# A retention layer with a gated MLP on one core: another hand-written order, and three kinds of copies that may run on GpSimd

## Chip, core and metric

One Trainium2 chip, of which the kernel uses one core. The metric is the device time of one execution in microseconds (us). The kernel before takes 418.49 us (median of three runs, 417.32 to 419.59).

## The reference, cut to what is computed

```python
# retention: batch 4, 8 heads, 768 positions, head size 64
gamma = 1.0 - 2.0 ** (-5.0 - np.arange(H))
for t in range(S):
    state = gamma * state + k[:, :, t] (outer) v[:, :, t]
    y[:, :, t] = D ** -0.5 * q[:, :, t] @ state
x = y laid out as (batch, position, 512)
# gated MLP
h = gelu_tanh(x @ w_in)                  # 512 -> 1024
u, v = h[..., :512], h[..., 512:]
v_n = (v - mean(v)) / sqrt(var(v) + 1e-6) * g_ln
v_s = einsum('ts,bsd->btd', w_sg, v_n) + b_sg[None, :, None]
out = x + (u * v_s) @ w_out
```

`q`, `k`, `v` and the vectors are float32, and three of the weight matrices (`w_in` in two halves, `w_out`) reach the core as 64-bit numbers.

## The kernel before

The work is cut by batch `b` (0 to 3), by half of the sequence `hf` (0 and 1, 384 positions each) and, in the retention, by pair of heads `p` (0 to 3). The retention of one (b, hf, p) goes through six chunks of 64 positions: key times value of each chunk (`D`, a_states), the scan over the chunk states on VectorE (`T`, a_scan, into the tile `sq`), key times query (`S`, a_scores), the mask (`M`, VectorE), the copy of the scanned states beside the queries (`W`, a_beside, two copies of 64 partitions each, into `mw`), the sum of both parts (`O`, a_out), and its scaling into the tile `x` (`X`, a_grow, VectorE). Each result is then split into a high part (`H`, a_hi, a cast) and a low part (`I`, a_lo, a subtraction), so that the MLP can run as three reduced-precision products in place of one. The MLP's steps are `V` and `v` (value half and its gelu), `s`, `N`, `n` (layer norm), `a` and `b` (its high and low parts), `U` and `u` (gate half and its gelu), `G` (the product over positions with `w_sg`), `e`, `m`, `h`, `j` (bias, gate, high and low parts), `Y` (product with `w_out`), `r` and `y` (residual, sum and store).

Weights are prepared on the core: `l` loads a piece, `k`, `b`, `r`, `a` turn a 64-bit piece into float32 (ScalarE, three VectorE instructions, ScalarE, GpSimd), and `h` and `o` split it into a high and a low part. The second letter of such a word names the matrix: `v`, `u` (halves of `w_in`), `o` (`w_out`), `s` (`w_sg`).

No scheduler runs: the list `PROG` is walked word by word, each word issues its step's instructions on their engines, and each engine executes its own in that order. So `X013` is a_grow of batch 0, second half, pair 3, and a last letter D, G or A names VectorE, GpSimd or ScalarE where a step has a choice. `~40` issues 40 matmuls on zeros that keep TensorE busy. All loads and stores are issued by SyncE in the order of `PROG`; the framework gives them eight semaphores in turn, so that each waits for the transfer eight places ahead of it.

Buffers matter in what follows. The PSUM tiles of `D`, `S` and `O` share four buffers; those of the MLP share four others. The tiles `x` and `sq` have one buffer each, so that the next `X` waits for the `I` of the one before, and the next `T` for the `W` of the one before. The key tile of all but the first four pairs has two buffers, so that its load waits for the `D` and `S` of two pairs earlier.

In the kernel before, `P` (scaling of the keys, L242), `W` (L143 by way of L288), `H` (L322) and the high parts of weights (L214) always run on ScalarE.

Of the kernel before, what the change touches and what calls it, by code (L numbers as in the profile page):

```python
# [43 lines left out]
av2 hv0 T000 rv1 W000 lu0 ov0D S001 ls0 bv1 L002 hv2 O000 P001 M001 K000 ov2G C010 D001 L003 ku2 X000 ru2 ~1  # L44
T001 av1 H000 S010 P010 W001 D010 bu2 ~2 L012 kv3 M010 K001 O001 I000G C011 hv1 ~2 T010 lo0 rv3 au2 V0010 lu1
ru3 X001 V0000 H001 bv3 W010 V0020 S011 I001D P011 ov1D O010 ku0 M011 av3 D011 hu2 X010 V0001 ru0 L013 ou2G
T011 H010 V0011 P002 V0021 Q W011 bu0 lo1 D002 I010G S002 hv3 T002 O011 P003 au0 M002 W002 S003 D003 X011 K002
M003 hu0 S012 H011 ou0G O002 T003 ro0 C012 P012 M012 I011G U0000 W003 ov3D D012 X002 K003 ru1 O003 T012 L100
H002 S013 ku1 I002D C013 W012 bu1 V0002 V0012 X003 au1 P013 V0022 M013 H003 D013 ku3 I003D O012 hu1 bu3 L101
ko1 U0001 ro1 X012 au3 ls5 P100 V0013 T013 ls1 H012 V0003 u000 ls6 ou1D v001 V0023 ls10 bo1 W013 lo2 U0010 ls7  # L50
s001 I012G U0020 lo3 v000 v002 ao1 s000 U0011 hs6 s002 hu3 U0021 os6G P101 N00 u001 ou3G ro2 O013 u002 D100
X013 ro3 D101 n000 H013 n001 S100 a000 T100 I013G a001 S101 L102 ko3 M100 b000G U0030 ko0 M101 ko2 ls2 K100
V0120 W100 b001D ls4 U0031 ls3 n002 bo0 L103 a002 V0121 u003 V0100 P102 b002D ls11 V0122 bo2 ls8 V0110 hs3 hs0
V0123 os3D hs2 bo3 V0111 hs9 v012 V0101 hs5 s012 os0G V0112 P103 T101 hs11 V0102 os9G hs1 V0113 hs8 os1D hs7
V0103 os8D v011 U0100 os2D hs4 v010 s011 os11G U0110 hs10 s010 W101 os5G U0120 N01 ao2 U0101 n011 U0121 n012
u010 n010 U0111 os10D a010 os4D u012 b010G U0130 u011 O100 os7G D102 ao0 X100 O101 H100 D103 I100D a011 S102
ao3 X101 ho0 H101 S103 M102 L110 b011G a012 V1020 ho3 M103 U0131 L111 ho1 b012G C110 ho2 V1000 u013 I101D
G0000 oo1D oo3D V1001 P110 oo0G V1021 G0010 K101 oo2G T103 C111 G0001 P111 W103 G0011 K103 G0002 T102 G0012
W102 K102 e000 m000G G0020 e001 m001G h000 G0120 j000G h001 G0021 j001D G0121 r000G G0022 r001G G0122 e002
m002G G0030 r002D h002 O102 j002G D110 X102 O103 H102 T110 D111 I102D S110 W110 X103 S111 M110 L112 H103 V1022  # L60
T111 C113 I103G C112 V1002 L113 M111 W111 G0031 V1023 V1003 v102 G0032 P112 s102 v100 G0100 s100 e003 P113
Y0000 m003G G0110 r003D h003 G0101 j003D Y0001 G0111 y000 G0102 G0112 e010 m010G Y0010 e011 m011G U1000 r010D
# [25 lines left out]
Y2021 M310 W311 V3003 y202 V3011 v300 Y2000 P312 s300 Y2030 P313 Y2001 Y2031 y200 V3012 y203 G2120 V3013 U3000
v301 s301 G2100 G2121 G2101 U3001 G2122 u300 V3020 G2102 V3021 e210 e211 O310 m210D D312 m211D O311 X310 T312
D313 H310 S312 I310D W312 r210D S313 X311 r211G M312 V3022 H311 Y2010 I311D T313 V3023 h210 M313 h211 Y2011  # L90
v302 j211G W313 G2130 s302 j210D U3010 N30 G2131 e212 U3011 n302 n300 G2132 n301 a300 m212D a301 y201 b300G
U3020 a302 e213 u301 Y2130 h212 b301D r212D V3100 b302G V3120 V3101 m213G V3121 j212G h213 U3021 j213D O312
u302 r213G O313 X312 H312 V3110 I312D Y2131 X313 H313 V3102 y213 V3111 I313D V3103 V3112 v310 V3122 s310 V3113
V3123 v311 U3100 s311 v312 s312 Y2120 N31 U3101 Y2121 u310 n312 n310 Y2110 n311 a310 y212 a311 b310G U3030
a312 Y2111 b311D b312G Y2100 y211 U3110 G3010 U3111 G3011 u311 G3030 G3012 G3031 Y2101 G3032 y210 G3000 U3031
G3001 u303 U3120 G3002 U3121 e300 e301 U3130 u312 m300D m301G h300 G3020 r300D h301 U3131 r301D j301D G3021
j300G u313 G3100 G3022 G3101 e302 e303 Y3020 m302D m303G h302 Y3030 r302D h303 G3102 j302G G3120 r303G e310
G3110 m310G G3121 j303G G3111 r310D Y3021 G3122 y302 Y3031 G3112 y303 Y3000 e311 m311D G3130 r311G Y3001 G3131
y300 Y3010 G3132 h310 h311 j310D Y3011 j311D e312 Y3100 e313 m312G y301 Y3120 m313D h312 r312G h313 Y3110
j313D Y3130 j312D r313G Y3121 Y3111 y312 Y3131 y311 Y3101 y313 y310  # L100
# [472 lines left out]
```

## Time and profile before

| | |
|---|---|
| median of three runs | 418.49 us |
| lowest and highest | 417.32 and 419.59 us |
| the profiled execution's own time | 419.46 us |
| span of its profile | 417.7 us |
| busy: TensorE, VectorE, ScalarE, GpSimd | 402.6, 234.4, 173.7, 149.9 us |
| mean granted TensorE clock | 0.988 |
| bytes moved | 41.38 MB |

The span is the time from the first to the last instruction; the 1.8 us between it and the execution's own time lie around it. "Busy" of TensorE counts matmuls from start to a modelled end, so that a busy TensorE need not run at its full rate. In the views, PE is TensorE's matmuls, PEld its weight loads, DVE VectorE, ACT ScalarE, POOL GpSimd, SP SyncE.

### The profile page before, as it was taken

How to read it: one execution, taken by the hardware profiler on the slowest of the kernel's cores; microseconds unless marked ns; L12 is line 12 of the kernel's file. 1: busy time of each engine (PE TensorE's matmuls, PEld its weight loads, DVE VectorE, ACT ScalarE, POOL GpSimd, SP SyncE). 2: the span in 40 equal slices, each digit the busy share in tenths (PEclk: the TensorE clock that was granted, in tenths of full speed). 3: DMA queues.
4: the chain of work that ended last, by engine and by line, in shares of the span. 5: the costliest groups of instructions: out<-in, count | busy, mean ns of one | idle time of the engine just before them, and what ended most of it. 6: DMA issues, size and time to landing. Idle time of an engine off the chain costs nothing.

```text
span 417.7 us, 9358 instructions
## 1 busy us (share of the span) xinstructions
PE 402.6 (96%) x3924; PEld 368.3 (88%) x3924; DVE 234.4 (56%) x461; ACT 173.7 (42%) x306; POOL 149.9 (36%) x148
## 2 busy tenths in 40 slices
PE   8987989969999999999999999999999999999996
PEld 3666878959999999899998999899999998999995
DVE  3897799973453473673454226464272694704453
ACT  4787878454350153544152324355161342201010
POOL 4553244384511513130670471214550042202521
PEclk9999999969999999999999999999999999999999
DMA  8999578040051161415060006225042000100012
GB/s 247 345 288 287 175 250 214 2 134 19 4 151 39 38 176 54 121 32 152 2 184 25 20 0 209 89 83 155 0 126 85 2 19 20 38 20 2 8 58 88
DMA packets 18122, 41.38 MB, mean 99 GB/s; under 512 B 2464, under 2 KB 8096, under 8 KB 18080
## 3 DMA queue, kind: packets, MB, share of 16 engines
q1 hardware_dynamic: 17936, 40.51, 32.4%
q8 instruction: 31, 0.51, 0.6%
q10 hardware_dynamic: 144, 0.27, 0.2%
q14 instruction: 11, 0.09, 0.1%
HBM read 34.48 MB, written 6.29 MB: 98 GB/s over the span
## 4 chain that ended last, share of the span: by engine, by line
PE 79%; DMA 8%; DVE 7%; issue 3%; POOL 1%; SPq 1%; ACT 0%; DVEq 0%; POOLq 0%
PE ps L412 24%; PE py L450 16%; PE pu L395 13%; PE pv L339 13%; PE po L306 5%; PE sc L263 4%; PE ds L255 4%; DMA kt<-in_kk_dram 3%; DMA raw<-in_w_v_dram 2%; DMA raw<-in_w_sg_dram 2%; DMA mw<-in_qv_dram 2%; POOL ws L218 1%; DVE mw L281 1%; DVE wx L179 1%; DVE wx L178 1%
## 5 line engine op out<-in xcount | busy, mean ns | idle before, releaser
L412 PE MATMUL ps<-ws,vh 128*128 128x384 f32 x576 | 106.9, 335 | 0.0
L412 PEld LDWEIGHTS ps<-ws,vh 128*128 128x128 f32 x576 | 100.8, 188 | 1.2
L339 PE MATMUL pv<-wv,xh 128*128 128x512 f32 x288 | 76.1, 402 | 0.0
L395 PE MATMUL pu<-xh,wu 128*128 128x384 f32 x384 | 75.5, 345 | 0.0
L450 PE MATMUL py<-gh,wo 128*128 128x384 f32 x384 | 73.5, 337 | 0.0
L395 PEld LDWEIGHTS pu<-xh,wu 128*128 128x128 f32 x384 | 69.5, 192 | 1.9 <-ACT v L349 0.4
L450 PEld LDWEIGHTS py<-gh,wo 128*128 128x128 f32 x384 | 67.1, 188 | 1.6 <-DVE o L465 0.2
L339 PEld LDWEIGHTS pv<-wv,xh 128*128 128x128 f32 x288 | 53.4, 190 | 10.5 <-ACT v L349 0.5
L143 ACT COPY mw<-sq 64x320 f32<-64x320 f32 (+1 forms) x64 | 52.6, 821 | 20.8 <-DVE sq L268 20.2
L422 DVE SCALAR_TENSOR_TENSOR gt<-ps,gb 128x384 f32<-128x384 f32 x32 | 19.1, 613 | 52.1 <-PE ps L412 49.9
L385 POOL TENSOR_TENSOR vh<-v,vh 128x512 fp32r<-128x512 f32 x19 | 25.0, 1341 | 57.1 <-ACT vh L381 57.1
L433 POOL TENSOR_TENSOR gt<-gt,u 128x384 f32<-128x384 f32 x23 | 24.6, 1073 | 54.6 <-DVE gt L422 54.5
L437 ACT CAST gh<-gt 128x384 fp32r<-128x384 f32 x32 | 16.4, 513 | 63.5 <-POOL gt L433 32.8
L281 DVE TENSOR_TENSOR mw<-sc,tab 64x384 f32<-64x384 f32 x64 | 35.5, 555 | 8.2 <-PE sc L263 5.1
L465 DVE TENSOR_TENSOR o<-py,o 128x384 f32<-128x384 f32 x32 | 17.3, 551 | 33.9 <-PE py L450 28.6
L263 PE MATMUL sc<-mw,kt 64*64 64x64 f32 x768 | 28.0, 222 | 7.3 <-DVE x L313 5.6
L405 ACT ACTIVATE u<-pu 128x384 f32<-128x384 f32 x32 | 15.3, 487 | 44.9 <-PE pu L395 44.6
L263 PEld LDWEIGHTS sc<-mw,kt 64*64 64x64 f32 x768 | 25.3, 137 | 9.8 <-DVE x L313 6.0
L268 DVE TENSOR_TENSOR_SCAN sq<-step,ds 128x384 f32<-128x384 f32 x32 | 30.2, 943 | 6.0 <-PE ds L255 4.1
L306 PEld LDWEIGHTS po<-mw 128*64 128x64 f32 (+1 forms) x768 | 27.0, 139 | 7.1 <-issue 4.7
L306 PE MATMUL po<-mw 128*64 128x64 f32 (+1 forms) x768 | 32.2, 229 | 0.9 <-issue 0.8
L313 DVE TENSOR_TENSOR x<-po,tab 128x384 f32<-128x384 f32 x32 | 17.6, 551 | 27.3 <-PE po L306 24.4
(56 smaller groups left out, 393.2 us busy)
## 6 DMA issues: line engine op xcount, KB each, us to landing
kt<-in_kk_dram SPq DMA_DIRECT2D x32, 384.0 KB, 5.0
mw<-in_qv_dram SPq DMA_DIRECT2D x64, 192.0 KB, 5.4
out_dram<-o SPq DMA_DIRECT2D x32, 192.0 KB, 1.8
raw<-in_w_sg_dram SPq DMA_DIRECT2D x12, 192.0 KB, 4.7
raw<-in_w_v_dram SPq DMA_DIRECT2D x4, 512.0 KB, 7.0
...
```

Of the source, the lines that this page charges most:

```text
L143: nc.scalar.copy(out=out, in_=in_)
L263: mm(out=scs[u][o, c], lhsT=kt[i, c], rhs=mv[j][i, c], start=True, stop=True)
L268: nc.vector.tensor_tensor_scan(out=sqs[u].rearrange("p e c -> p (e c)"), data0=step_t[:, p].rearrange("p e c -> p (e c)"), data1=dss.pop(u ...
L281: nc.vector.tensor_tensor(out=mv[j][h], in0=sc[h], in1=mask_t[h, p : p + 1, :].to_broadcast([64, NCH, C]), op=ALU.mult,)
L306: mm(out=pos[u][o, c], lhsT=w[j][i, c], rhs=mv[j][i, c], start=True, stop=True)
L339: mm(out=pv[b, hf, k], lhsT=x[:, p, a, k * 128 : (k + 1) * 128], rhs=wv_t[:, w, p], start=(p == 0 and n == 0), stop=(p == NP - 1 and n == 2),)
L385: engines[e].tensor_tensor(out=h[:, 1], in0=vt.pop((b, hf, k)), in1=h[:, 0].bitcast(F32), op=ALU.subtract)
L395: mm(out=pu[b, hf, f], lhsT=wu_t[:, w, f, p * 128 : (p + 1) * 128], rhs=x[:, p, a], start=(n == 0), stop=(n == 11),)
L412: mm(out=ps[b, hf, d], lhsT=vh[b, t][:, v, d * 128 : (d + 1) * 128], rhs=ws_t[hf * NT + t][:, w], start=(n == 0), stop=(n == 3 * NT - 1),)
L422: nc.vector.scalar_tensor_tensor(out=t, in0=ps.pop((b, hf, d)), scalar=g_t[:, d : d + 1], in1=b_t[:, hf * HT : (hf + 1) * HT], op0=ALU.mul ...
L433: engines[e].tensor_tensor(out=t, in0=t, in1=ut.pop((b, hf, d)), op=ALU.mult)
L450: mm(out=py[b, hf, c], lhsT=wo_t[c][:, w, d * 128 : (d + 1) * 128], rhs=gh[b, hf, d][:, a], start=(d == 0 and n == 0), stop=(d == 3 and n ...
```

## The change

`PROG` is a new list with the same steps and the same tile sizes: each matmul, load and vector operation of before is in it once. Five places of matmuls on zeros hold 40, 9, 8, 1 and 10 in place of 40, 7, 1, 2 and 2. `P`, `W`, `H` and the weights' `h` now carry an engine. Of 32 key scalings 6 go to GpSimd, of 64 half copies `W` (now one word for each half) 20, of 32 `H` 10, of the weights' 24 high parts 4. Steps that had a choice before are dealt out anew: on VectorE now stand 14 `I` (13 before), 12 `b` (5), 14 `m` (9), 19 `j` (11), 16 `r` (14), 9 low parts of `w_sg` (6), 3 of the gate half (1) and 2 of the value half (3), with the rest of each on GpSimd. A step `Z`, which would issue half a load from ScalarE's queue, is written but stands nowhere in the list.

```diff
-~40 lv0 R lv2 L000 lv1 L001 rv0 kv0 rv2 bv0 lu2 kv2 L010 bv2 ls9 P000 S000 av0 lv3 D000 lu3 M000 kv1 ~7 L011
+~40 lv0 R lv2 L000 lv3 L001 rv0 kv2 rv2 bv2 L010 kv0 bv0 P000A lu2 S000 av2 D000 M000 kv3 ~9 av0 rv3 T000 L011
...
+ON_ACT = {tuple(int(c) for c in w[1:]) for w in PROG if w[0] == "Z"}
...
-    def w_hi(m, i):
+    def w_hi(m, i, e):
...
-        nc.scalar.copy(out=w_parts(m, i)[0], in_=wx[m, i])
+        copy(e, w_parts(m, i)[0], wx[m, i])
...
-        for j, m in enumerate((m0, m1)):
-            h = slice(64 * j, 64 * j + 64)
-            nc.sync.dma_start(out=m[h].rearrange("p a c t -> p (a c t)"), in_=qv[b, hf, p, h])
+        ms[u] = m0, m1
+        for j in (0,) if u in ON_ACT else (0, 1):
+            a_load_half(nc.sync, j, *u)
...
-    def a_keys(*u):
-        ks = kts[u][1]
-        nc.scalar.activation(out=ks, in_=ks, func=AF.Copy, scale=vec_t[:, 0, u[2] : u[2] + 1])
+    def a_load_half(queue, j, b, hf, p):
+        h = slice(64 * j, 64 * j + 64)
+        queue.dma_start(out=ms[b, hf, p][j][h].rearrange("p a c t -> p (a c t)"), in_=qv[b, hf, p, h])
+
+    def a_load_rest(*u):
+        a_load_half(nc.scalar, 1, *u)
+
+    def a_keys(b, hf, p, e):
+        ks, by = kts[b, hf, p][1], vec_t[:, 0, p : p + 1]
+        if e == "A":
+            nc.scalar.activation(out=ks, in_=ks, func=AF.Copy, scale=by)
+        else:
+            engines[e].tensor_scalar(out=ks, in0=ks, scalar1=by, scalar2=None, op0=ALU.mult)
...
-    def a_beside(b, hf, p, e="A"):
-        u = b, hf, p
-        for j in range(2):
-            h = slice(64 * j, 64 * j + 64)
-            copy(e, mws[u][1][j][h, 1 - hf :].rearrange("p c e -> p e c"), sqs[u][h, :, : NCH - 1 + hf])
+    def a_beside(b, hf, p, j, e):
+        u, h = (b, hf, p), slice(64 * j, 64 * j + 64)
+        copy(e, mws[u][1][j][h, 1 - hf :].rearrange("p c e -> p e c"), sqs[u][h, :, : NCH - 1 + hf])
...
-    def a_hi(*u):
-        b, hf, p = u
-        nc.scalar.copy(out=xn[b, hf][:, p, 0], in_=xs[u])
+    def a_hi(b, hf, p, e):
+        copy(e, xn[b, hf][:, p, 0], xs[b, hf, p])
```

Three places of the new order matter below.

The first is SyncE's queue, from the load of pair (0, 1, 2) on (`kt` holds keys, `mw` queries and values, `raw` weights, and `gb` the gate's constants). Before:

```order
L233 DMA kt_334<-in_kk_dram 128x768
L236 DMA mw_335<-in_qv_dram 64x768
L236 DMA mw_336<-in_qv_dram 64x768
L164 DMA raw_367<-in_w_out_dram 128x512
L164 DMA raw_375<-in_w_u_dram 128x512
L233 DMA kt_446<-in_kk_dram 128x768
L236 DMA mw_447<-in_qv_dram 64x768
L236 DMA mw_448<-in_qv_dram 64x768
L490 DMA gb_71<-in_gb_dram 128x772
L164 DMA raw_469<-in_w_out_dram 128x512
```

The same place in the changed kernel, where L238 and L247 are the lines of `kt` and `mw`, and L169 that of weights:

```order
L238 DMA kt_414<-in_kk_dram 128x768
L247 DMA mw_415<-in_qv_dram 64x768
L247 DMA mw_416<-in_qv_dram 64x768
L238 DMA kt_441<-in_kk_dram 128x768
L247 DMA mw_442<-in_qv_dram 64x768
L247 DMA mw_443<-in_qv_dram 64x768
L169 DMA raw_495<-in_w_sg_dram 128x384
L169 DMA raw_513<-in_w_out_dram 128x512
L169 DMA raw_534<-in_w_u_dram 128x512
L238 DMA kt_648<-in_kk_dram 128x768
```

The load of the last pair of batch 0 has moved ahead of two 512 KB pieces of weights.

The second place is VectorE around `X013` (its row is `x<-po`), whose reading of PSUM frees the buffer that `S101` on TensorE takes. Before:

```order
L370 SCALAR_TENSOR_TENSOR lny_805<-lnt_806,lny_805 128x3
L313 TENSOR_TENSOR x_851<-po_823,tab_70 128x384
L375 TENSOR_SCALAR v_776<-v_776,mvar_764,lny_805 128x512
L375 TENSOR_SCALAR v_740<-v_740,mvar_764,lny_805 128x512
L268 SCALAR_TENSOR_TENSOR sq_885<-step_75,ds_838 128x384
L281 TENSOR_TENSOR mw_631<-sc_870,tab_70 64x384
```

After (`lny` is the last instruction of the layer norm's 12 small ones, `v` are its `n`, `wx` the conversion of two pieces of `w_out`, `ws` a low part of `w_sg`):

```order
L382 SCALAR_TENSOR_TENSOR lny_820<-lnt_821,lny_820 128x3
L387 TENSOR_SCALAR v_788<-v_788,mvar_775,lny_820 128x512
L387 TENSOR_SCALAR v_771<-v_771,mvar_775,lny_820 128x512
L387 TENSOR_SCALAR v_763<-v_763,mvar_775,lny_820 128x512
L183 TENSOR_SCALAR wx_852<-wx_852 128x512
L184 TENSOR_SCALAR wx_852<-wx_852 128x512
L187 SCALAR_TENSOR_TENSOR wx_852<-raw_737,wx_852 128x512
L183 TENSOR_SCALAR wx_869<-wx_869 128x512
L184 TENSOR_SCALAR wx_869<-wx_869 128x512
L187 SCALAR_TENSOR_TENSOR wx_869<-raw_731,wx_869 128x512
L223 TENSOR_TENSOR ws_877<-raw_495,ws_877 128x384
L326 TENSOR_TENSOR x_917<-po_884,tab_70 128x384
```

Three `n`, six conversions and one low part of `w_sg` now stand between the small ones and `X013`, where before nothing did.

The third place is VectorE at `X100` and `X101`, the first and second pair of batch 1. Before:

```order
L313 TENSOR_TENSOR x_1162<-po_1133,tab_70 128x384
L326 TENSOR_TENSOR xh_1161<-x_1162,xh_1161 128x384
L313 TENSOR_TENSOR x_1208<-po_1164,tab_70 128x384
L281 TENSOR_TENSOR mw_904<-sc_1194,tab_70 64x384
L281 TENSOR_TENSOR mw_905<-sc_1194,tab_70 64x384
L281 TENSOR_TENSOR mw_950<-sc_1213,tab_70 64x384
L281 TENSOR_TENSOR mw_951<-sc_1213,tab_70 64x384
L326 TENSOR_TENSOR xh_1161<-x_1208,xh_1161 128x384
```

After (L326 is now the line of `X`, L283 that of the scan `T`, here `T102`, L397 the norm's low parts `b`, L338 `I100`, L296 the masks):

```order
L326 TENSOR_TENSOR x_1193<-po_1160,tab_70 128x384
L283 SCALAR_TENSOR_TENSOR sq_1210<-step_75,ds_1177 128x384
L397 TENSOR_TENSOR vh_1227<-v_1046,vh_1227 128x512
L397 TENSOR_TENSOR vh_1195<-v_1069,vh_1195 128x512
L338 TENSOR_TENSOR xh_1192<-x_1193,xh_1192 128x384
L296 TENSOR_TENSOR mw_997<-sc_1245,tab_70 64x384
L296 TENSOR_TENSOR mw_998<-sc_1245,tab_70 64x384
L326 TENSOR_TENSOR x_1290<-po_1197,tab_70 128x384
```

The scan `T102` has moved up to right behind `X100`, and `S103` on TensorE, which took the PSUM buffer that `X101` frees, now takes the one that `T102` frees.

## Rows read from the trace of the kernel before

**Rows 1.** The page: span and busy time of each engine.

```profile
span 417.7 us, 9358 instructions
PE 402.6 (96%) x3924; PEld 368.3 (88%) x3924; DVE 234.4 (56%) x461; ACT 173.7 (42%) x306; POOL 149.9 (36%) x148
```

**Rows 2.** Busy time by stretch: PE, PEld, DVE, ACT, POOL; clock, DMA share, GB/s.

```profile
0.00:85.27 85.27, 77.03 (x966) 60.69 (x966) 69.85 (x133) 60.11 (x107) 36.77 (x39) 0.98 0.75 221
85.27:94.94 9.67, 6.61 (x61) 5.92 (x62) 6.83 (x10) 5.03 (x12) 9.67 (x9) 0.65 0.57 165
94.94:144.93 49.99, 49.99 (x387) 47.88 (x385) 22.17 (x37) 15.83 (x28) 17.27 (x18) 1.00 0.16 49
144.93:413.98 269.05, 268.94 (x2514) 253.82 (x2513) 134.99 (x283) 92.70 (x161) 86.18 (x85) 1.00 0.23 67
```

**Rows 3.** Timeline of TensorE: start, length, instruction [idle before, what ended it].

```profile
32.17 0.91 PE L255 MATMUL ds<-mw,kt 64*64 64x64 f32 x24 [1.39 <-DMA mw<-in_qv_dram]
...
61.89 0.92 PE L263 MATMUL sc<-mw,kt 64*64 64x64 f32 x24 [1.58 <-DVE x L313]
...
85.32 0.92 PE L263 MATMUL sc<-mw,kt 64*64 64x64 f32 x24 [1.00 <-DVE x L313]
89.24 1.54 PE L263 MATMUL sc<-mw,kt 64*64 64x64 f32 x24 [3.01 <-DVE x L313]
...
94.94 0.34 PE L412 MATMUL ps<-ws,vh 128*128 128x384 f32 x1
```

**Rows 4.** Timelines of VectorE and ScalarE around `X013`, `X100` and `X101`.

```profile
61.28 0.56 DVE L313 TENSOR_TENSOR x<-po,tab 128x384 f32<-128x384 f32 x1
...
84.72 0.55 DVE L313 TENSOR_TENSOR x<-po,tab 128x384 f32<-128x384 f32 x1
...
86.91 0.51 ACT L322 CAST xh<-x 128x384 fp32r<-128x384 f32 x1 [1.57 <-POOL ws L218]
...
87.45 1.07 DVE L326 TENSOR_TENSOR xh<-x,xh 128x384 fp32r<-128x384 f32 x1 [2.19 <-ACT xh L322]
88.63 0.56 DVE L313 TENSOR_TENSOR x<-po,tab 128x384 f32<-128x384 f32 x1
```

**Rows 5.** Groups up to 85.27 us: busy us, mean ns | idle before, what ended it.

```profile
L339 PE MATMUL pv<-wv,xh 128*128 128x512 f32 x72 | 18.1, 400 | 0.0
L281 DVE TENSOR_TENSOR mw<-sc,tab 64x384 f32<-64x384 f32 x20 | 11.1, 555 | 3.0 <-DMA mw<-in_qv_dram 1.6 <-PE sc L263 0.9
L268 DVE TENSOR_TENSOR_SCAN sq<-step,ds 128x384 f32<-128x384 f32 x10 | 9.4, 942 | 2.8 <-PE ds L255 2.6
L178 DVE TENSOR_SCALAR wx<-wx 128x512 f32<-128x512 f32 x12 | 6.6, 553 | 6.0 <-ACT wx L170 6.0
L313 DVE TENSOR_TENSOR x<-po,tab 128x384 f32<-128x384 f32 x9 | 4.9, 544 | 0.9 <-PE po L306 0.9
L218 DVE TENSOR_TENSOR ws<-raw,ws 128x384 fp32r<-128x384 f32 x6 | 3.5, 620 | 0.0
L326 DVE TENSOR_TENSOR xh<-x,xh 128x384 fp32r<-128x384 f32 x3 | 1.6, 541 | 0.0
```

**Rows 6.** Groups over the whole span: copies, and the matmuls of `G`.

```profile
L412 PE MATMUL ps<-ws,vh 128*128 128x384 f32 x576 | 106.9, 335 | 0.0
...
L143 ACT COPY mw<-sq 64x384 f32<-64x384 f32 x32 | 28.2, 880 | 7.9 <-DVE sq L268 7.5
...
L145 POOL COPY cy<-sq 128x64 f32<-128x64 f32 x16 | 6.3, 393 | 17.1 <-DVE sq L268 17.0
...
L484 POOL COPY step<-tab 128x1280 f32<-128x1280 f32 x1 | 1.3, 1258 | 4.0 <-DMA tab<-in_c_tab_dram 4.0
```

**Rows 7.** Timeline of GpSimd and VectorE, 9 to 11 us, and VectorE 8.

```profile
7.75 0.43 DVE L179 TENSOR_SCALAR wx<-wx 128x512 int32<-128x512 int32 x1
...
9.04 1.41 POOL L197 TENSOR_TENSOR wx<-wx,raw 128x512 int32<-128x512 int32 x1 [1.60 <-DVE wx L182]
...
9.33 1.40 DVE L179 TENSOR_SCALAR wx<-wx 128x512 int32<-128x512 int32 x1
```

More of the change, by code (lines that the diff above doesn't have):

```diff
@@ L42 @@
 PROG = """
-~40 lv0 R lv2 L000 lv1 L001 rv0 kv0 rv2 bv0 lu2 kv2 L010 bv2 ls9 P000 S000 av0 lv3 D000 lu3 M000 kv1 ~7 L011
[L44 to L62, printed above, removed]
@@ L88 @@
[L88 to L97, printed above, removed]
@@ L98 @@
[L98 to L100 removed]
+~40 lv0 R lv2 L000 lv3 L001 rv0 kv2 rv2 bv2 L010 kv0 bv0 P000A lu2 S000 av2 D000 M000 kv3 ~9 av0 rv3 T000 L011
+hv2A W0000A bv3 hv0A lv1 S001 P001A ov0D W0001A D001 ls10 ov2G M001 O000 lu0 av3 X000 P010A lu3 S010 H000A ~8
@@ new lines @@
+K000 hv3A M010 ku2 ov3G T001 ru2 L002 C010 bu2 D010 W0011A ~1 P011A S011 I000D W0010A K001 L003 V0000 au2 M011
+C011 kv1 V0010 rv1 T010 V0020 hu2A bv1 W0100A D011 O001 ku0 ou2D L012 ~10 ru0 bu0 ru3 ku3 X001 av1 W0101A L013
+P002A S002 T011 H001G hv1A D002 M002 W0111A au0 O010 ls0 W0110A I001D hu0A S003 lo3 ov1D P003A O011 X010 ou0G
+lu1 T002 H010A D003 I010G M003 W0020A U0000 W0021A bu3 V0001 P012A V0021 X011 K002 au3 V0011 C012 T003 H011A
+P013A S012 W0030A I011D O002 W0031G M012 hu3A D012 ro3 K003 S013 X002 L100 C013 ou3D H002A O003 ku1 T012 I002G
@@ new lines @@
+D013 ru1 ls9 M013 W0120G W0121A V0012 ls5 ls11 X003 V0002 L101 bu1 H003A V0022 O012 I003D lo2 T013 au1 P100A
+lo0 U0001 hs9A ls4 X012 W0131A hs0G V0023 ls1 ls6 hu1A V0013 os9D v002 V0003 ou1D ls8 v001 s002 os0G U0100
+u000 ls3 v000 s001 hs5G U0010 H012A ls2 s000 P101A W0130A I012D U0020 lo1 N00 os5G ro2 U0030 ro0 ls7 n000
+U0011 ko0 n001 a000 n002 U0031 bo0 a001 ko2 U0021 hs3A bo2 hs11A O013 u003 hs1A os3D D100 hs10A X013 b000G
+u002 D101 H013A T100 S100 hs4A b001G hs2A S101 u001 M100 L102 ko1 K100 V0120 ko3 ao2 M101 V0110 L103 ro1 V0121
@@ new lines @@
+hs8A I013D a002 os1D V0111 Q hs6A os10D V0122 hs7A b002D W1001A U0101 os7D os4D P102A V0123 bo1 u010 V0112
+v012 os8D V0100 W1000A s012 os2G V0113 T101 P103A V0101 ao1 v011 U0110 W1011A s011 K101 ho1A ao0 V0102 W1010A
+U0120 os11D os6D V0103 bo3 U0130 v010 s010 ho0G U0121 N01 U0131 oo1G u012 U0111 u013 n011 n012 O100 u011 n010
+ao3 D102 a010 X100 a011 O101 T102 H100A b010G D103 a012 ho2A S102 b012D S103 b011D L110 I100D G0020 M103 ho3G
+L111 G0000 X101 C110 oo0G M102 C111 G0021 oo3D G0001 H101G G0022 P110A oo2D G0002 I101G V1020 K102 e000 W1021G
@@ new lines @@
+G0010 P111A m000D V1021 W1020G h000 G0011 j000D T103 r000G V1000 G0012 W1031A K103 W1030G V1001 e001 e002 O102
+m001G D110 X102 m002G h001 O103 T110 D111 H102G h002 S110 W1100A j001D S111 W1101G M110 L112 G0030 M111 j002G
+C113 L113 G0110 T111 I102G C112 G0031 W1110A r001D X103 r002G W1111A V1022 V1002 H103G G0032 P112G G0111 e003
+I103D Y0000 m003G P113A V1023 h003 r003G V1003 v102 j003G G0112 s102 v100 s100 Y0001 G0100 y000 G0120 G0101
+G0121 G0102 G0122 e010 e011 U1000 m010D m011D Y0010 r010D r011G U1001 G0130 u100 Y0020 Y0011 Y0021 y001 V1010
@@ L218, in w_lo @@
         engines[e].tensor_tensor(out=lo, in0=wx.pop((m, i)), in1=hi.bitcast(F32), op=ALU.subtract)
-    kts, mws, dss, scs, sqs, pos, carry, xs, xn = {}, {}, {}, {}, {}, {}, {}, {}, {}
+    kts, mws, dss, scs, sqs, pos, carry, xs, xn, ms = ({} for _ in range(10))
     def a_load(*u):
```

66 lines of the change are left out of this document (40 added, 26 removed).

## The prediction

> **What bounds the kernel now.** I read first the page, then the busy time by stretch, then the timelines around TensorE's waits. On the page [rows 1] TensorE is busy for 402.6 of 417.7 us, so at most some 15 us of plain waiting are there to win. The stretches say where [rows 2]: from 94.94 us to 413.98 it is busy for all but 0.1 us, so that whatever ScalarE, VectorE or GpSimd do better there can hardly show. The waiting lies in the first 94.94 us: 8.2 us up to 85.27 (85.27 - 77.03) and 3.1 us in the next 9.67. In these same 9.67 us the mean granted clock is 0.65, which is a mix of the 2.4 and the 1.2 GHz level; TensorE had stood idle for 3 us just before [rows 3].
>
> In that first part VectorE is the engine that others wait for. It is busy for 69.85 of 85.27 us, ScalarE for 60.11, GpSimd for 36.77 [rows 2]. TensorE's scores wait for VectorE's `x` at 61.89, 85.32 and 89.24 [rows 3], that is for `X013`, `X100` and `X101`, which end at 61.84, 85.27 and 89.19 [rows 4] and free PSUM buffers. The third is the dearest: `X101` could not run until `I100` had left the single `x` buffer, `I100` waited 2.19 us for ScalarE's `H100`, and that stood until a low part of `w_sg` on GpSimd had freed the tile it writes [rows 4]. Once, at 32.17, TensorE waits for a load [rows 3].
>
> A point at which both orders can be compared is the start of the first `G`. Before, it is at 94.94. The changed order has by then done the same matmuls, but for `V1020` and `V1000` (six of 512 columns, which at 18.1 us for 72 [rows 5] are 1.5 us) and with 16 more on zeros. So the changed kernel gains as much as its first `G` starts before 93.4 us.
>
> **The change, part by part.** *VectorE up to `X100`.* Counted word by word, the new order puts three more `I` (541 ns) and three more low parts of `w_sg` (620 ns) ahead of `X100` [rows 5]; one more low part of a 512-wide weight and one less of the norm's cancel. That is 1.6 + 1.9 = 3.5 us more, 73.4 busy in place of 69.85. Its idle time was 15.4 us: 6.0 before the first conversion, 3.0 before masks, 2.8 before scans, 0.9 before `X` [rows 5], and so 2.7 at the very start and in small pieces. The 6.0, the 2.7 and 1.6 of the masks' (a load) stay: 10.3. The other 5.1 were spent where VectorE had run out of work while the loads of pairs (0,1,2) and (0,1,3) and their copies came in. The new order asks for these before 1 MB of other weights, and puts two conversions, three `n` and two low parts of `w_sg`, which came after `X013`, ahead of it. I let 3.5 of the 5.1 go: 11.9 idle. `X100` then ends at 73.4 + 11.9 = 85.3, where it was. The ends are 83.7 (all 5.1 gone) and 88.8 (15.4 as before).
>
> *From `X100` to the first `G`.* `S102` still takes `X100`'s buffer, but `S103` now takes that of `T102`, which stands right behind `X100`: 942 ns [rows 5]. So `T102` ends at 86.2, `S103` runs for 0.9 us as at 85.32 [rows 3], and `G` starts at 87.1, against 93.4: a gain of 6.3 us, between 7.9 and 2.8 at the two ends. `X101`, `H101` (now GpSimd) and `I101` move behind, beside six parts of `G`. Nothing of the clock is counted beyond this; it comes with the hole.
>
> *Copies off ScalarE.* 20 half copies at 880 ns or less [rows 6], 6 scalings, 10 high parts and 4 of weights leave ScalarE, some 27 us. By themselves I cost them at nothing: ScalarE is busy for 60 of 85 us and far less later [rows 2], and no wait of TensorE in rows 3 is for it. What hides them is VectorE's longer queue. Were ScalarE's copies in the way after all, a pair of halves split over two engines would take one copy's time in place of two, 0.9 us less; up to `X100` that is `W003` and `W012`, 1.8 us.
>
> *Copies on GpSimd.* No row shows a half copy there. 1280 elements took 1258 ns in line, 64 strided ones out of the same `sq` 393 ns [rows 6]. For 384 elements that is 0.38 us at one end and 2.36 at the other; I take 1.0, in the middle by ratio, since a half copy reads in line and writes with a stride. The tightest early place is `O103`: GpSimd has `H101`, `I101`, `W1021`, `W1020`, then, as `sq` has one buffer, `T103` on VectorE, and `W1030`. With `X101` at about 89.8 (`T102`, two norm parts, `I100`, one mask pair and itself) and 1.0 to 1.1 each, `W1030` ends at about 97; TensorE comes to `O103` after nine parts of `G` (six matmuls at 106.9/576 us [rows 6], 1.1 each), 12 matmuls of `V` at 0.25 and two small steps, at 101 to 102. At 2.36 a copy this slack of four us is just used up. In the last batch `D313` and `O313` have come within 6 us of each other, with two GpSimd copies, a high and a low part between. For these and other places I take 1.5 us of loss after the first `G`, within -1 (the busy rows hide small waits, so a little could be won) and 4.
>
> *The zeros.* 16 more matmuls at about 0.25 us, as for the 512 columns of `V` [rows 5], are 4 us, ahead of `S001`, `D010` and `S002`, where TensorE waits for copies or for the load that it waits for at 32.17 [rows 3]. Up to `S102` TensorE has 8.2 us to spare [rows 2]; these 4 and one part of `U` that came later before (1.2) leave 3. I cost them at nothing; if that cover goes they cost up to 4.
>
> *Loads.* SyncE already waits for the transfer eight places ahead, in both orders, so no more are open; `Z` is not in the list. What is moved is worth what stands under VectorE's idle time. Behind the load of (1,0,0), which waits for `D012`, now stand three `w_sg` pieces, and behind (1,0,1), which waits for `D013`, two `w_out` pieces whose conversion stands ahead of `X013`.
>
> Sum: -6.3 + 1.5 = -4.8 us. The profiled execution took 419.46 us (span 417.7, 1.8 around it) and would take 414.7; it is 1.0 above the median of 418.49, so the median comes to **413.7 us**.
>
> **The rivals.** *A, larger gain.* VectorE's idle time falls to 10.3 and it is held up less by GpSimd, which has some three two-input operations less ahead of `X100`; one such cost it 0.97 us (1.40 against 0.43 [rows 7]). `X100` then ends at 83.7 - 2.2 = 81.5, which is as early as TensorE can follow, `G` starts at 83.3 and 10 us are won: 408.5. For it: the copies of a pair now run on two engines. Against it: 3 us more on the engine that bounds.
>
> *B, given back.* The work put ahead of `X013` only makes `S101` wait longer, VectorE idles as before, `X100` ends at 88.8, 2.8 us are won and 2 lost in the later places: 417.7. For it: VectorE does not get shorter work, and `w_out` now lies behind `D013`.
>
> *C, slower: GpSimd's copies hold VectorE.* While GpSimd added, a VectorE instruction of 0.43 us took 1.40 [rows 7]. If each moved copy does this too, the six ahead of `X100` (`H001`, `W0031`, `W0120`, `hs0`, `hs5`, `ho0`) cost 5.8 us: `X100` at 91.1, `G` at 92.9, 0.5 won; with half copies near 2.36 us, `O103` and the last batch lose 3.5. That is 421.5. It decides from about 1 us of hold for each copy and 2 us for the copy itself. Against it: the one copy in line [rows 6] is fast. The Trainium skill (GPSIMD Engine Reference, Key points) says that GpSimd shares its SBUF interfaces with VectorE and contends with VectorE instructions that use both ports or have two SBUF inputs; by that rule C's hold is real, the sum would be 421.5, and the pair in rows 7 agrees with it for a GpSimd addition, while no run here shows it for a copy.
>
> **How the numbers follow.** Forecast 0.45 (411 to 416.4 of its own), A 0.15, B 0.25, C 0.15. The range has to take in most of B, A at its edge and the nearer part of C: 408.5 to 420. Over 0.5% (2.1 us, about what a measurement of this kernel can tell from no change) means under 416.4 or over 420.6. Faster: nearly all of the forecast, A and a little of B, 0.61; same: most of B and the edge of C, 0.24; slower 0.15.
>
> **What would show it.** In the changed profile `X013` should end later than 61.84 and `S101` wait for it longer than 1.58 us, `X100` end near 85, `S103` no longer wait for `X101`, `G` start near 87 without a stretch at clock 0.65 before it, and TensorE be busy throughout from there. A half copy on GpSimd near 1.0 us confirms that price; above 2, or VectorE's sum up to `X100` above 76 us, speaks for C. The forecast is wrong if `X100` ends after 89, or if over 3 us are lost after the first `G`.

## The result and the profile after

The changed kernel takes **414.71 us** (median of four runs, 414.46 to 414.90) against 418.85 us for the kernel before on the same chip (417.32 to 419.59, four runs). The ratio is 0.9905, with a 95% interval from 0.9876 to 0.9935: faster by 0.95%, where 413.7 us was forecast. The profiled execution took 414.86 us, its span is 413.1 us. When the changed kernel ran again beside later experiments, one of its seven executions took 436.19 us at a mean granted clock of 0.852; the row "changed, again" below leaves it out, and its trace serves only to show how far two traces of one kernel differ (its `X100` ends at 85.13).

The page of the changed kernel, beside [rows 1]: VectorE's busy time has grown by 12.7 us, ScalarE's has shrunk by 27.1.

```profile
span 413.1 us, 9386 instructions
PE 400.7 (97%) x3937; PEld 366.1 (89%) x3940; DVE 247.1 (60%) x488; ACT 146.6 (35%) x266; POOL 155.2 (38%) x161
```

Busy time by stretch, columns as in [rows 2]. The cuts are the end of `X100` (87.30), the first `G` (89.05) and the start of `O110` (140.54):

```profile
0.00:87.30 87.30, 79.54 (x985) 61.54 (x988) 72.39 (x140) 57.92 (x104) 39.46 (x43) 1.00 0.73 217
87.30:89.05 1.75, 1.70 (x48) 1.56 (x48) 0.94 (x2) 1.75 (x5) 1.49 (x2) 1.00 0.00 0
89.05:140.54 51.49, 51.49 (x395) 49.18 (x391) 27.87 (x46) 12.28 (x23) 27.14 (x28) 1.00 0.26 78
140.54:413.00 272.46, 267.98 (x2514) 253.86 (x2513) 145.87 (x303) 74.62 (x136) 87.16 (x89) 1.00 0.22 68
```

The stretch from `X100` to the first `G`, 9.67 us at a granted clock of 0.65 before [rows 2], is now 1.75 us at 1.00. The stretch ahead of it is longer in this trace: `X100` ends at 87.30 in place of 85.27. That difference is no larger than the one between two traces of the changed kernel (87.30 and 85.13).

TensorE's timeline at `S100` and `S101`, and at `S102`, `S103` and the first `G` (columns as in [rows 3]):

```profile
62.45 0.87 PE L278 MATMUL sc<-mw,kt 64*64 64x64 f32 x24
66.23 0.91 PE L278 MATMUL sc<-mw,kt 64*64 64x64 f32 x24 [2.91 <-DVE x L326]
...
87.35 1.77 PE L278 MATMUL sc<-mw,kt 64*64 64x64 f32 x48 [0.70 <-DVE x L326]
89.05 3.21 PE L424 MATMUL ps<-ws,vh 128*128 128x384 f32 x17
```

VectorE's timeline at `X013`, and at `X100`, `T102` and what follows:

```profile
65.62 0.55 DVE L326 TENSOR_TENSOR x<-po,tab 128x384 f32<-128x384 f32 x1
...
86.75 0.55 DVE L326 TENSOR_TENSOR x<-po,tab 128x384 f32<-128x384 f32 x1
87.21 0.94 DVE L283 TENSOR_TENSOR_SCAN sq<-step,ds 128x384 f32<-128x384 f32 x1
88.97 2.66 DVE L397 TENSOR_TENSOR vh<-v,vh 128x512 fp32r<-128x512 f32 x2 [0.81 <-ACT vh L393]
```

`S102` and `S103` are one row of 48 matmuls now. `S103` follows `T102` and no longer `X101`. `S101` waits longer than in [rows 3], 2.91 us in place of 1.58, for the later `X013`.

VectorE's waits up to the end of `X100`, longest sums first, in the kernel before and then in the changed one (instruction, what it waited for: us in total, times, longest):

```profile
DVE wx L178 <- ACT wx L170: 6.0, 1, 6.0
DVE sq L268 <- PE ds L255: 2.6, 2, 2.4
DVE mw L281 <- DMA mw<-in_qv_dram: 1.6, 1, 1.6
DVE mw L281 <- PE sc L263: 0.9, 1, 0.9
```

```profile
DVE wx L183 <- ACT wx L175: 6.8, 1, 6.8
DVE mw L296 <- PE sc L278: 3.5, 5, 1.6
...
DVE ws L223 <- ACT ws L148: 0.7, 1, 0.7
DVE wu L223 <- ACT wu L148: 0.5, 1, 0.5
```

The waits of the scans and of the load are gone. The wait for TensorE's scores has grown from 0.9 to 3.5 us, and waits of 1.2 us for high parts made by ScalarE have come up. Idle time is 15.4 us before (85.27 - 69.85) and 14.9 after (87.30 - 72.39).

### The profile page after: what moved, and what is told of

The parts are those of the page before. It is cut to its first block, busy times and chain, and to the rows that moved or that the text cites. A ratio compares the mean times of both kernels' runs of the same rounds, so it can differ in the third digit from the quotient of the medians.

```text
span 413.1 us, 9386 instructions
## 1 busy us (share of the span) xinstructions
PE 400.7 (97%) x3937; PEld 366.1 (89%) x3940; DVE 247.1 (60%) x488; ACT 146.6 (35%) x266; POOL 155.2 (38%) x161
## 4 chain that ended last, share of the span: by engine, by line
PE 78%; DVE 9%; DMA 9%; issue 1%; ACT 1%; SPq 0%; ACTq 0%
PE ps L424 24%; PE py L462 16%; PE pv L351 13%; PE pu L407 13%; PE po L319 5%; DMA mw<-in_qv_dram 5%; PE sc L278 4%; PE ds L270 4%; DMA raw<-in_w_v_dram 2%; DMA tab<-in_c_tab_dram 1%; DMA raw<-in_w_sg_dram 1%; DVE ws L223 1%; DVE st L365 1%; DVE wx L187 1%; DVE mw L296 1%
## 5 line engine op out<-in xcount | busy, mean ns | idle before, releaser
L424 PE MATMUL ps<-ws,vh 128*128 128x384 f32 x576 | 105.7, 336 | 0.0
L407 PE MATMUL pu<-xh,wu 128*128 128x384 f32 x384 | 73.0, 339 | 1.6 <-DVE gt L434 1.1
L351 PE MATMUL pv<-wv,xh 128*128 128x512 f32 x288 | 74.1, 396 | 0.0
L462 PE MATMUL py<-gh,wo 128*128 128x384 f32 x384 | 72.1, 336 | 0.0
L407 PEld LDWEIGHTS pu<-xh,wu 128*128 128x128 f32 x384 | 67.5, 188 | 3.8 <-DVE gt L434 1.4
L148 ACT COPY mw<-sq 64x320 f32<-64x320 f32 (+1 forms) x44 | 36.2, 822 | 29.9 <-DVE sq L283 29.6
L296 DVE TENSOR_TENSOR mw<-sc,tab 64x384 f32<-64x384 f32 x64 | 35.5, 555 | 9.4 <-PE sc L278 7.9
L365 DVE BATCH_NORM_STATS2 st<-v 128x6 f32<-128x512 f32 x24 | 16.4, 683 | 31.4 <-ACT v L361 31.4
L473 POOL TENSOR_TENSOR o<-xh 128x384 f32<-128x384 f32 x16 | 18.0, 1125 | 40.6 <-DVE gt L445 40.3
L326 DVE TENSOR_TENSOR x<-po,tab 128x384 f32<-128x384 f32 x32 | 17.6, 549 | 25.0 <-PE po L319 20.4
L283 DVE TENSOR_TENSOR_SCAN sq<-step,ds 128x384 f32<-128x384 f32 x32 | 30.1, 941 | 2.3 <-PE ds L270 1.6
L445 POOL TENSOR_TENSOR gt<-gt,u 128x384 f32<-128x384 f32 x18 | 19.2, 1071 | 31.7 <-DVE gt L434 31.7
L319 PE MATMUL po<-mw 128*64 128x64 f32 (+1 forms) x768 | 31.0, 226 | 0.0
```

Of the source, the lines that this page charges most:

```text
L148: nc.scalar.copy(out=out, in_=in_)
L283: nc.vector.tensor_tensor_scan(out=sqs[u].rearrange("p e c -> p (e c)"), data0=step_t[:, p].rearrange("p e c -> p (e c)"), data1=dss.pop(u ...
L296: nc.vector.tensor_tensor(out=mv[j][h], in0=sc[h], in1=mask_t[h, p : p + 1, :].to_broadcast([64, NCH, C]), op=ALU.mult,)
L319: mm(out=pos[u][o, c], lhsT=w[j][i, c], rhs=mv[j][i, c], start=True, stop=True)
L351: mm(out=pv[b, hf, k], lhsT=x[:, p, a, k * 128 : (k + 1) * 128], rhs=wv_t[:, w, p], start=(p == 0 and n == 0), stop=(p == NP - 1 and n == 2),)
L365: nc.vector.bn_stats(out=st, in_=vt[b, hf, k])
```

## The experiments

The ratio is against runs of the kernel before on the same chip; e1 to e4 shared one chip, e5 to e8 another, and e9 to e11 a third, on which the changed kernel ran again. "Stretch" is worked out from the trace: for each form of VectorE instruction I took the duration that only a tenth of its instructions undercut, over all these traces, and summed what the instructions up to `X100` took beyond it. A trace is one execution of a kernel whose runs lie up to 5 us apart, so times of `G` and `X100` tell apart less finely than they look: the two traces of the changed kernel have `X100` 2.2 us apart. The four traces of the new order with `X100` ahead of 86 us (e1, e4, e9, e10) are of the fastest or the second fastest of six executions each, so that an early `X100` need not be the work of the edit.

| run | ratio to before (95%) | median us | first `G` | `X100` ends | VectorE busy up to `X100` | stretch |
|---|---|---|---|---|---|---|
| before | 1 | 418.85 | 94.94 | 85.27 | 69.85 | 9.9 |
| changed | 0.9905 (0.9876-0.9935) | 414.71 | 89.05 | 87.30 | 72.39 | 9.9 |
| changed, again | 0.9901 (0.9866-0.9936) | 414.28 | - | - | - | - |
| e1 copies back | 0.9837 (0.9802-0.9871) | 413.71 | 87.46 | 85.70 | 70.89 | 8.4 |
| e2 scan early | 0.9992 (0.9960-1.0023) | 419.70 | 96.78 | 86.59 | 71.49 | 11.5 |
| e3 scan late | 1.0005 (0.9977-1.0034) | 420.68 | 93.75 | 86.78 | 72.36 | 9.7 |
| e4 weights late | 0.9895 (0.9849-0.9941) | 415.36 | 87.47 | 85.71 | 70.31 | 7.6 |
| e5 more on VectorE | 0.9943 (0.9917-0.9969) | 417.19 | 92.15 | 90.29 | 75.12 | 10.5 |
| e6 more on ScalarE | 0.9903 (0.9875-0.9931) | 415.29 | 89.92 | 88.16 | 72.33 | 9.9 |
| e7 zeros back | 0.9899 (0.9868-0.9931) | 414.80 | 88.78 | 86.91 | 72.89 | 10.3 |
| e8 low parts to GpSimd | 0.9918 (0.9886-0.9949) | 415.52 | 90.03 | 88.27 | 72.78 | 12.0 |
| e9 load late | 0.9908 (0.9872-0.9944) | 415.06 | 87.84 | 85.98 | 71.20 | 8.6 |
| e10 to VectorE | 0.9907 (0.9871-0.9944) | 415.22 | 86.76 | 85.00 | 71.20 | 5.8 |
| e11 together | 0.9881 (0.9848-0.9914) | 413.92 | 88.13 | 86.37 | 69.61 | 5.2 |

> The changed kernel once more, as the row that the other runs of this chip stand beside: 413.9 to 415.5 us, first chunk product within 1 us of 89 us.

### The third place, undone and alone: e3 and e2

```diff
-X100 a011 O101 T102 H100A b010G D103 a012 ho2A S102 b012D S103 b011D L110 I100D G0020 M103 ho3G L111 G0000 X101 C110
+X100 a011 O101 H100A b010G D103 a012 ho2A S102 b012D b011D L110 I100D X101 S103 T102 G0020 M103 ho3G L111 G0000 C110
```

> The changed kernel with the third place undone: T102 stands behind the high and low parts of chunk 100 again, and S103 waits for X101. Theory: S103 starts near 92.8 us in place of 88.2, the first chunk product near 93.6 in place of 89.05, time 4 to 5 us above the changed kernel (about 419 us). Rival (what S103 waits for is hidden by zeros or caught up later): time within 1 us of the changed kernel.

The ratio is 0.010 above the changed kernel's, some 4.2 us, as the theory has it (by the medians, of two chips, it is 6.0 us): with everything else of the change left in, the whole gain is gone. TensorE of e3 and its second stretch, columns as above:

```profile
92.27 1.55 PE L277 MATMUL sc<-mw,kt 64*64 64x64 f32 x24 [4.25 <-DVE x L325]
93.75 4.43 PE L423 MATMUL ps<-ws,vh 128*128 128x384 f32 x16
```

```profile
86.78:93.75 6.97, 2.71 (x69) 2.46 (x63) 4.52 (x6) 2.38 (x6) 4.88 (x5) 0.73 0.37 116
```

`S103` waits 4.25 us for `X101`, and behind that idle time it runs in 1.55 us in place of 0.87 to 0.91: the granted clock of the stretch is 0.73, a mix of the 2.4 and the 1.2 GHz level.

e2 is the counterpart: the order of before with one thing moved.

```diff
-X100 O101 H100 ... K101 oo2G T103 ... G0002 T102 G0012 W102 K102 e000
+X100 K101 T102 O101 H100 ... oo2G W102 K102 T103 ... G0002 G0012 e000
```

> The order of the kernel before, with one thing from the change: the keys of the last scan step and the step itself (T102) stand right behind X100, ahead of X101. Theory (the third place alone brings a part of the gain, since S103 then takes the buffer that T102 leaves and not the one that X101 leaves): S103 2 to 4 us earlier, time 414.5 to 417 us. Rival (the order of these few steps is worth nothing, the earlier X100 or the clock brings all): time within 0.7 us of the kernel before.

The rival's number came, but not for its reason. VectorE of e2 at `X100` and `T102`, then its GpSimd:

```profile
86.04 0.55 DVE L312 TENSOR_TENSOR x<-po,tab 128x384 f32<-128x384 f32 x1
89.70 0.95 DVE L267 TENSOR_TENSOR_SCAN sq<-step,ds 128x384 f32<-128x384 f32 x1 [3.11 <-POOL cy L144]
```

```profile
85.97 1.28 POOL L384 TENSOR_TENSOR vh<-v,vh 128x512 fp32r<-128x512 f32 x1 [9.86 <-ACT vh L380]
87.21 0.99 POOL L217 TENSOR_TENSOR ws<-raw,ws 128x384 fp32r<-128x384 f32 x1
88.16 1.28 POOL L196 TENSOR_TENSOR wx<-wx,raw 128x512 int32<-128x512 int32 x1
89.38 0.29 POOL L144 COPY cy<-sq 128x64 f32<-128x64 f32 x1
```

`T102` writes the one `sq` tile, which `K101` (the copy into `cy`) must have read. `K101` takes 0.29 us, but GpSimd works off three two-input operations first, the earliest of which waits for a high part. In the changed kernel `K101` is long done:

```profile
76.26 0.30 POOL L150 COPY cy<-sq 128x64 f32<-128x64 f32 x1 [0.56 <-DVE sq L283]
```

So e2 does not price the third place alone. It shows that the early `T102` needs `K101` ahead of GpSimd's batch of low parts, which the new order also brings.

### Which engine bounds the time up to `X100`: e5 and e6

```diff
-        engines[e].tensor_tensor(out=lo, in0=wx.pop((m, i)), in1=hi.bitcast(F32), op=ALU.subtract)
+        raw_in = wx.pop((m, i))
+        for _ in range(3 if (m, i) in (("s", 9), ("s", 3)) else 1):
+            engines[e].tensor_tensor(out=lo, in0=raw_in, in1=hi.bitcast(F32), op=ALU.subtract)
```

> The changed kernel with two of VectorE's low parts of weights (os9, os3) made three times each: four instructions of 0.55 to 0.6 us more on VectorE ahead of X100, 2.2 us in all (the output is the same). Theory (VectorE bounds up to X100): X100 and the first chunk product 1.5 to 2.3 us later, time 1.5 to 2.5 us above the changed kernel. Rival (VectorE's idle time takes the extra work in): less than 0.7 us.

The ratio rose by 0.004, 1.6 to 1.8 us, about as much as the intervals can tell; beside e6 and e7 on the same chip, the medians are 1.9 and 2.4 us higher. In the trace VectorE is busy for 2.7 us more (2.1 of them the new work, the rest stretch), `X100` and `G` are 3.0 and 3.1 us later. VectorE does bound: e6, with as much more work on ScalarE, shows no such rise.

In e6 it is the high part that is made three times:

```diff
-        copy(e, w_parts(m, i)[0], wx[m, i])
+        for _ in range(3 if (m, i) in (("s", 9), ("s", 3)) else 1):
+            copy(e, w_parts(m, i)[0], wx[m, i])
```

> The changed kernel with two casts of weights on ScalarE (hs9, hs3) made three times each: four instructions of 0.51 us more on ScalarE ahead of X100, 2.0 us in all (the output is the same). Theory (ScalarE does not bound): time within 0.7 us of the changed kernel; up to 1 us more only if the low part that waits for hs9 is pushed. Rival (ScalarE is now the bound): 1.5 to 2.3 us more.

The ratio did not move. The push is seen: VectorE's low part waits 3.2 us for ScalarE in place of 0.7, but its masks wait 1.3 us in place of 3.5.

```profile
DVE ws L224 <- ACT ws L148: 3.2, 1, 3.2
DVE mw L297 <- PE sc L279: 1.3, 2, 0.8
```

A wait of VectorE for ScalarE there mostly takes the place of one for TensorE. The two sorts cannot be added up as if each were time lost.

### Work ahead of `X013`, the load, the zeros: e4, e9, e7

```diff
-U0031 bo0 a001 ko2 U0021 hs3A bo2 hs11A O013 u003 hs1A os3D D100 hs10A X013 ... S101 u001 M100
+U0031 a001 ko2 U0021 hs3A hs11A O013 u003 hs1A D100 hs10A X013 ... S101 u001 M100 bo0 bo2 os3D
```

> The changed kernel with two weight casts and one low part (bo0, bo2, os3) moved from ahead of X013 to behind the mask of chunk 100. Theory (VectorE's sum up to X100 counts, not where in it X013 lies): S101's wait of 2.9 us falls to under 1 us, but X100 still ends within 0.7 us of 87.3 and the time stays within 0.7 us of the changed kernel. Rival (the wait of S101 is time lost): time 2 to 3 us below the changed kernel.

`S101`'s wait is gone:

```profile
60.59 1.57 PE L278 MATMUL sc<-mw,kt 64*64 64x64 f32 x48
```

The ratio is that of the changed kernel within its interval, and the median is 0.7 us higher, so no part of the 2.9 us shows as time lost; the interval (0.9849 at the least) leaves room for 2.3 us. The trace's `X100` is 1.6 us earlier, more than the theory allows, with the same 140 instructions: VectorE's stretch is 2.3 us smaller, which led to e10 below. The profiled execution was the fastest of six.

```diff
-W0101A L013 P002A S002 ... lo3 lu1
+W0101A lo3 lu1 L013 P002A S002 ...
```

> The changed kernel with one load put back: that of chunk 013's keys and mask starts behind two weight loads (lo3, lu1) again. Theory (the load order is worth what is in VectorE's idle time ahead of X100): D013 and S013 2 to 3 us later, of which 1 to 2 us reach X100 and the time. Rival (the load has slack, or VectorE makes up for it with other work): D013 within 1 us, time within 0.7 us of the changed kernel.

The rival holds: `D013` starts at 44.26 (44.91 in the changed kernel), the ratio is the same. The two parts of that load that carry `q` and `v` are issued 1.7 and 0.8 us later (33.40 and 34.20 in place of 31.70 and 33.39), and there was slack for that. This tests one load of the new order, not all.

```diff
-~40 ~9 ~8 ~1 ~10
+~40 ~7 ~1 ~2 ~2
```

> The changed kernel with the counts of zero products of the kernel before (52 in all in place of 68). Theory (the zeros fill waits and cost nothing): time within 0.5 us of the changed kernel and a granted clock of 1.00 up to the first chunk product. Rival 1 (the longer batches hold up scores behind them): 1 to 2 us less. Rival 2 (without them the clock falls before the first product, as in the kernel before): a stretch at about half clock and 1 to 3 us more.

The time stays, but the clock does not, where the theory had it at 1.00. The clock rows (40 slices, tenths of full speed) of the pages of e7 and then of e8, which has the zeros of the changed kernel; in the changed kernel all 40 digits are 9:

```profile
PEclk9969998999999999999999999999999999999999
```

```profile
PEclk9999998999999999999999999999999999999999
```

In e7 the clock falls twice ahead of the first `G`: in the third slice, behind 2.32 us without a matmul ahead of `S002`, and in the seventh, behind 2.66 us ahead of `S101`. Only the first can be the work of the missing zeros. The second is also on the pages of e5, e8 and e9, where `S101` waits for 4.43, 2.11 and 2.23 us and then takes 1.54 to 1.55 us, while in the changed kernel it waits for 2.91 us and takes 0.91. Why the same wait takes the clock down in some traces and not in others is open. In the time nothing shows of either fall: rival 2 had the fall, but not its price.

### Copies back on ScalarE: e1

```diff
-H001G ... W0031G ... W0120G ... hs0G ... ho0G ... H101G ... W1021G ... P112G
+H001A ... W0031A ... W0120A ... hs0A ... ho0A ... H101A ... W1021A ... P112A
```

(All forty `P`, `W`, `H` and `h` words that end in G end in A.)

> The new order and loads stay, but all forty key scalings, state copies and high parts that had gone to GpSimd run on ScalarE again. Theory (VectorE's work up to X100 sets the start of the chunk products, and ScalarE has room): first chunk product within 1 us of the changed kernel's 89.05 us, time 413.7 to 415.7 us against its 414.7. Rival (the gain comes from taking 27 us of copies off ScalarE): first product back towards 93 us and time near 418 us.

Theory, and a little beyond it (the first `G` is 1.6 us earlier, where 1 us was allowed): this is the fastest kernel run, at ratio 0.9837, 1.0 us below the changed kernel by the medians and 2.8 by the ratios (the changed kernel did not run on that chip, so I give both). The copies on GpSimd brought nothing and seem to have cost something. The trace has `X100` 1.6 us earlier, VectorE's stretch 1.5 us smaller; whether that is the cause is one trace's word.

### What stretches VectorE: e8, e10, e11

```diff
-os1D os10D os7D os4D
+os1G os10G os7G os4G
```

> The changed kernel with four more low parts of weights (os1, os10, os7, os4, some 0.55 us each) moved from VectorE to GpSimd. Theory (VectorE's sum counts): VectorE is relieved of 2.2 us ahead of X100, of which 1 to 2 us reach the first chunk product, time 1 to 2 us below the changed kernel. Rival (two-input work on GpSimd holds VectorE, whose masks beside it take 1.5 to 1.65 us in place of 0.95 to 1.1): the stretches give it back, time 0 to 1 us above.

The rival's number came, 0.5 us above the changed kernel by the ratios. VectorE has four instructions less, 2.1 us of undisturbed work, and is as busy as in the changed kernel (72.78 and 72.39 us): its stretch grew by 2.1 us. The rival named the wrong instructions, though. No mask of any trace takes over 0.57 us; what is held most are the conversions, as e10 shows.

```profile
0.00:88.27 88.27, 80.76 (x988) 62.76 (x988) 72.78 (x136) 58.05 (x104) 44.98 (x47) 0.98 0.74 214
```

The opposite, e10, moves six low parts from GpSimd to VectorE:

```diff
-os0G os5G os2G b000G b001G oo1G
+os0D os5D os2D b000D b001D oo1D
```

> The changed kernel with six low parts that GpSimd made ahead of X100 (os0, os5, os2, b000, b001, oo1) made by VectorE. They are 0.53 to 0.67 us each there, 3.6 us in all. Theory (VectorE's SBUF work stands still beside GpSimd's two-input work, which these six are: VectorE's stretches beside them summed to some 4.8 us in the changed kernel): VectorE's busy time up to X100 falls by 0 to 1.5 us in spite of six more instructions, time 0 to 1.5 us below the changed kernel. Rival (the stretches come from something else, so VectorE simply has 3.6 us more to do): busy time 3 to 4 us more, time 2 to 4 us above.

```profile
0.00:85.00 85.00, 78.65 (x985) 61.24 (x988) 71.20 (x146) 57.52 (x104) 32.60 (x37) 1.00 0.76 222
```

VectorE does six instructions more (3.6 us undisturbed) and is busy for 1.2 us less: its stretch fell from 9.9 to 5.8 us. Where it comes from can be read off three instructions. VectorE and then GpSimd of the changed kernel while `b000` and `b001` run on GpSimd (L397):

```profile
60.19 0.42 DVE L183 TENSOR_SCALAR wx<-wx 128x512 f32<-128x512 f32 x1
60.65 1.39 DVE L184 TENSOR_SCALAR wx<-wx 128x512 int32<-128x512 int32 x1
62.07 1.65 DVE L187 SCALAR_TENSOR_TENSOR wx<-raw,wx 128x512 int32<-128x512 int32 x1
```

```profile
60.14 3.02 POOL L397 TENSOR_TENSOR vh<-v,vh 128x512 fp32r<-128x512 f32 x2 [7.01 <-ACT vh L393]
```

And VectorE of e10, where GpSimd has nothing to do at that point:

```profile
58.68 0.42 DVE L182 TENSOR_SCALAR wx<-wx 128x512 f32<-128x512 f32 x1
59.13 0.43 DVE L183 TENSOR_SCALAR wx<-wx 128x512 int32<-128x512 int32 x1
59.60 0.69 DVE L186 SCALAR_TENSOR_TENSOR wx<-raw,wx 128x512 int32<-128x512 int32 x1
```

1.39 and 1.65 us become 0.43 and 0.69. So the theory holds for VectorE's work, and the rival's 3 to 4 us more of it did not come. The time is another matter: 415.22 us beside 414.28 on the same chip. The rival's 2 to 4 us more lie outside e10's own interval (0.9944 at the most, 1.8 us above "changed, again"), and a gain is not seen; the trace, with its early `X100`, is of the fastest of six executions, 2.7 us below their median.

e11 puts e1, e4 and four of e10's six together:

```diff
-os0G os5G os2G oo1G, forty copies on G, bo0 bo2 os3D ahead of X013
+os0D os5D os2D oo1D, forty copies on A, bo0 bo2 os3D behind M100
```

> A version meant to be faster: the changed kernel with all forty copies back on ScalarE, with bo0, bo2 and os3 behind the mask of chunk 100, and with os0, os5, os2 and oo1 made by VectorE (b000 and b001 stay with GpSimd). Theory (two single steps of 1 to 1.6 us each in the span, which overlap in part, and 0 to 0.7 us from the low parts): first chunk product at 85.5 to 87.5 us, time 1.5 to 3.5 us below the changed kernel (411 to 413 us). Rival (each of the single steps only shifted what GpSimd's work fell beside, and together they shift it back): within 1 us of the changed kernel.

VectorE's busy time fell by 2.8 us to 69.61, but its idle time rose from 14.9 to 16.8, and 0.9 us are left at the first `G`. The ratio of 0.9881 is 0.002 below the changed kernel's on the same chip, with intervals that overlap: the hoped-for 1.5 us or more is not seen, and the rival's "within 1 us" is what came. In this trace VectorE has less to do and waits longer for the others; the gain of single steps did not add up.

## Why the prediction was right, point by point

**VectorE's sum up to `X100`: right, 1.0 us too large.** Forecast 73.4 us busy, measured 72.39. The undisturbed work grew from 64.0 to 67.2 us, by 3.2 where 3.5 were counted word by word, and the stretch stayed (9.9 both times); rival A needed it to shrink. (The records of neighbouring instructions overlap a little, so that work and stretch add up to more than the busy time.)

**VectorE's idle time: too small by 3.0 us, the term that failed.** I let 3.5 of 5.1 us of waiting go, since the loads and copies behind them were asked for earlier. The 2.6 us at scans did go, and so did the 1.6 us at a load, which I had left in the sum. But the waits for scores grew by 2.6 us, to 3.5 in five places, 1.2 for high parts of weights came up, and 0.8 more before the first conversion: 14.9 in place of 11.9. This is more than one trace's word: in no trace of the table does VectorE idle for less than 13.8 us up to `X100` (e10). Rival B had this half right: VectorE idles as before. e6 shows how such waits replace one another.

**`X100` to the first `G`: right to 0.1 us.** Forecast `X100` plus 0.9 for `T102` plus 0.9 for `S103`, 1.8; measured 1.75. The stretch at a clock of 0.65 is gone. Against the break-even of 93.44 the first `G` won 4.4 us in place of 6.3, and the missing 1.9 are the later `X100` (87.30 in place of 85.3): 3.0 us more idle time, less the 1.0 us by which the sum was too large. As the other trace of the changed kernel has 85.13, a part of this may belong to the trace and not to the kernel.

**After the first `G`: forecast a loss of 1.5 us, measured none.** The last part of `Y` starts at 412.73 us before and at 408.42 after, 4.3 earlier, so 0.1 of the 4.4 were lost. The half copies on GpSimd took less than the 1.0 us assumed. Groups of GpSimd in the changed kernel, columns as in [rows 5]:

```profile
L150 POOL COPY mw<-sq 64x384 f32<-64x384 f32 x11 | 9.8, 888 | 6.5 <-DVE sq L283 6.3
L257 POOL TENSOR_SCALAR kt<-kt,tab 128x384 f32<-128x384 f32 x6 | 7.8, 1297 | 6.7 <-DMA kt<-in_kk_dram 3.9 <-DMA mw<-in_qv_dram 2.5 <-PE pv L351 0.3
...
L150 POOL COPY mw<-sq 64x320 f32<-64x320 f32 x9 | 7.6, 842 | 3.8 <-PE py L462 3.4
...
L150 POOL CAST xh<-x 128x384 fp32r<-128x384 f32 x10 | 5.1, 505 | 26.7 <-DVE x L326 26.7
```

The two errors, 1.9 and 1.4 us, cancel in part, which is luck: -4.3 in place of -4.8.

**Copies worth nothing, zeros and loads too.** e7 and e9 agree for the zeros and for the one load tried. For the copies e1 says nothing or a small cost: the sign of C, not its size. C's mechanism, a hold of VectorE by each moved copy, is not in the traces as far as they reach. Up to 88 us, VectorE instructions that work in SBUF lay beside one-input copies of GpSimd alone for some 7.4 us in ten traces (before, changed, e1 to e8) and took 0.35 us longer, but these are nearly all `K` copies into `cy`; a moved copy is in it with 0.13 us. Over the whole span and all traces of the table, VectorE's TENSOR_TENSOR with both inputs in SBUF lay beside half copies alone for 10.1 us and beside key scalings for 6.6, and took 0.4 us longer in each case, while beside two-input operations it took 140 us longer in 331. (Beside casts it is 0.4 in 1.1, of two instructions, too few to tell.) A moved copy beside one of VectorE's conversions, as in C's example, is not tested. The pair in [rows 7] was an addition, with two inputs.

It is GpSimd's copy that gets longer. Half copies beside such instructions alone took 3.3 us longer in 8.9, and a `K` copy, which takes 0.29 to 0.30 us by itself, takes up to 1.01 beside VectorE's work in SBUF; in the kernel before (shortest, median and longest in ns):

```profile
L145 POOL COPY cy<-sq x16: 285/300/1006, 15.1 to 288.3; 128x64 f32<-128x64 f32 x16
```

**Which part of the change brought the gain.** e3 settles that the third place is needed: without it the changed kernel is no faster than the one before. e2 shows that it is not enough by itself: in the old order `T102` waits for `K101`. That the third place and an early `K101` would do in the old order was not run.
